# The taps of a short convolution, laid out once per partition by the host

## The chip, the cores and the metric

One core of one Trainium2 chip runs the program. The metric is device time in microseconds for one execution of the whole program, as the median of several runs. Preparing the input arrays on the host is not part of it.

## The reference

The sequence has 2048 positions of 576 channels. Two kinds of layers alternate, each of them twice, and each adds its result to its input. The first kind is a Fourier mixing over channels and positions; the second is a short causal convolution of four taps over the keys, a product with the values, a long causal convolution (2048 taps for each channel) and a gate. Everything is in 32-bit floats.

```python
def _A_ref(x, dft_seq_re, dft_seq_im, dft_hid_re, dft_hid_im):
    a = jnp.einsum("bsd,ed->bse", x, dft_hid_re)
    b = jnp.einsum("bsd,ed->bse", x, dft_hid_im)
    return jnp.einsum("ts,bse->bte", dft_seq_re, a) - jnp.einsum("ts,bse->bte", dft_seq_im, b)

def _B_ref(q, k, v, shift_k, ssm_k, ssm_D):
    k_pad = jnp.pad(k, ((0, 0), (ks - 1, 0), (0, 0)))
    k_shift = jnp.zeros_like(k)
    for t in range(ks):                       # ks = 4
        k_shift = k_shift + k_pad[:, t:t + S, :] * shift_k[:, ks - 1 - t][None, None, :]
    kv = k_shift * v
    ...                                       # y: long convolution of kv with ssm_k
    y = y + kv * ssm_D[None, None, :]
    return q * y

x = x + _A_ref(_layernorm(x), ...)
x = x + _B_ref(_layernorm(x), B_k, B_v, B_shift_k, B_ssm_k, B_ssm_D)
x = x + _A_ref(_layernorm(x), ...)
x = x + _B_ref(_layernorm(x), B_k, B_v, B_shift_k, B_ssm_k, B_ssm_D)
```

## The kernel before

The long convolution's result does not depend on the layers' input, only on the keys, the values and the filters. So the kernel computes it once, in pieces, beside the matrix products of the first Fourier layer.

**The Fourier layer.** `layer` walks over steps: for each of four blocks of 512 output positions, for the real and the imaginary matrix, and for each of 16 blocks of 128 input positions, one step. A step takes a 256 KB slice of the sequence matrix (`load_c`, issued through `load_after`, line 159, on SP's queue two steps ahead), splits it into a high and a low part (ScalarE on line 91, VectorE on line 92), and multiplies it with one block of normalized rows: twelve matmuls into four PSUM accumulators named `s` and two into one named `rm`, all on line 74. The rows come from `get_x0`: a load on SP (line 646), statistics on VectorE (line 172) or ScalarE (lines 612 and 614), the scaling on ScalarE (line 182, or 639 from the ninth block on), and the split by `to_x` (line 186 on ScalarE, 188 and 189 on VectorE).

**The branch.** `branch` is a generator for the long convolution; the main loop takes pieces from it between the steps. Its first stage goes over 16 blocks of keys times values and 16 blocks of the filter. `f1_loads` fetches the blocks, `f1_split` splits one (lines 91 and 92), and `f1_products` multiplies it with a constant matrix: four groups of three matmuls, each into a bank of a ring of three (`bk`), each evicted by ScalarE (line 432) and, two at a time, stored from ScalarE's queue (line 433).

**The short convolution.** `convolve`, a generator inside `branch`, runs on VectorE: for each pair of blocks and each of the four taps one product (line 382), and from the second tap on a sum (line 387). The padded keys are loaded by `load_k` (line 361, 4,608 bytes a partition, a partition's rows 36,864 bytes apart). The taps are loaded once, by `load_w4` (line 353) when `convolve` is first asked for work: two loads of two taps each, on SP's queue. Their destination is a tile of 1,152 words on each of the 128 partitions, the same 4,608 bytes on each, because every partition needs all channels of both taps. The tile lies in the region named `f1f` in the profile. The taps then stay there for the whole first stage.

**What sets the order.** Each engine executes its own instructions in order, and the order is fixed when the program is built; semaphores make an instruction wait for its inputs and for the space it writes to. SP issues most loads, ScalarE's queue the stores, GpSimd's queue a few loads that convert a type. Loads that one queue issues are served in the order of issue, so a load that is served slowly holds up those behind it.

Of the kernel before, what the change touches and what calls it, by code (L numbers as in the profile page):

```python
# [15 lines left out]
P = 128  # L16
S = 2048
D = 576
# [46 lines left out]
def fnet_h3_kernel(ctx: ExitStack, tc: tile.TileContext, x, c_mat, w_re, w_im, k_pad, v, shift_k,  # L65
                   ssm_k, ssm_d, f1c, i2c, midc, out):
    nc = tc.nc
# [68 lines left out]
    def two(v):  # L136
        return v.rearrange("p (a n) -> p a n", a=2)
# [200 lines left out]
    def branch():  # L338
# [11 lines left out]
        def load_w4():  # L350
            for i in range(2):
                t = two(ring["wt"]())
                nc.sync.dma_start(t, bass.AP(tensor=shift_k.tensor, offset=shift_k.offset + 2 * i * D,
                                             ap=[[0, P], [D, 2], [1, D]]))
                wt.extend(t[:, i, :].unsqueeze(1).broadcast_to([P, 2, D]) for i in range(2))

        def load_k(upto):
# [15 lines left out]
        def convolve():  # L373
            for i in range(J // 2):
                if not wt:
                    load_w4()
                load_k(i + KR - 1)
                rp = rows[i] = two(ring["rp"]())
                for t in range(4):
                    out_t = two(tmp) if t else rp  # L380
                    for n, k in k_rows(2 * i + t):
                        nc.vector.tensor_tensor(out_t[:, n], k, wt[3 - t][:, n], OP.mult)
                    yield
                    if t == 1:
                        load_k(i + KR)
                    if t:
                        nc.vector.tensor_tensor(rp, rp, out_t, OP.add)
                        yield
# [716 lines left out]
```

## Time and profile before

| | |
|---|---|
| median of three runs | 1205.37 us (1202.85, 1205.37, 1206.05) |
| span of the profiled execution | 1202.1 us |
| mean granted TensorE clock | 0.997 |
| DMA, mean over the span | 218 GB/s, 261.95 MB |
| SP's queue (q1), share of 16 engines | 53.2% |
| ScalarE's queue (q10), share of 16 engines | 10.2% |
| tap loads | 2 of 576.0 KB each, from SP |

The span runs from the first to the last instruction of one profiled execution; all times in the profile count from its start. The median stands 3.3 us above it. In the rows of the windows, columns name the busy time and number of instructions of each engine in a stretch, then the clock that TensorE was granted as a share of full speed, the mean busy share of the 16 DMA engines (above 1 where packets overlap) and the rate. In rows of the timeline, the brackets give the engine's idle time before the instruction and what ended it. `PEld` are TensorE's weight loads; `q` behind an engine's name is its sequencer, which issues DMAs. Durations of matmuls in the timeline are modelled and overlap; the chain of waits does not count an overlap twice.

### The profile page before, as it was taken

How to read it: one execution, taken by the hardware profiler on the slowest of the kernel's cores; microseconds unless marked ns; L12 is line 12 of the kernel's file. 1: busy time of each engine (PE TensorE's matmuls, PEld its weight loads, DVE VectorE, ACT ScalarE, POOL GpSimd, SP SyncE). 2: the span in 40 equal slices, each digit the busy share in tenths (PEclk: the TensorE clock that was granted, in tenths of full speed). 3: DMA queues.
4: the chain of work that ended last, by engine and by line, in shares of the span. 5: the costliest groups of instructions: out<-in, count | busy, mean ns of one | idle time of the engine just before them, and what ended most of it. 6: DMA issues, size and time to landing. Idle time of an engine off the chain costs nothing.

```text
span 1202.1 us, 18251 instructions
## 1 busy us (share of the span) xinstructions
PE 1181.4 (98%) x6320; PEld 1026.7 (85%) x6320; DVE 840.0 (70%) x1498; ACT 666.5 (55%) x1335; POOL 74.1 (6%) x116
## 2 busy tenths in 40 slices
PE   7999999999999999999999999999999999999997
PEld 5888888988888888888988898888888888789997
DVE  7899983678777677675347766775776777774764
ACT  6965665669877768675435666544444445450210
POOL 2200000000000000001101121000000000001111
PEclk9999999999999999999999999999999999999999
DMA  9879898546656666648967686872682686794621
GB/s 337 288 235 306 289 295 260 180 139 178 216 178 200 211 180 202 189 147 244 307 204 237 221 257 211 272 266 72 215 283 71 205 286 220 265 352 143 219 95 40
DMA packets 146110, 261.95 MB, mean 218 GB/s; under 512 B 15841, under 2 KB 44769, under 8 KB 146018
## 3 DMA queue, kind: packets, MB, share of 16 engines
q1 hardware_dynamic: 102674, 205.58, 53.2%
q10 hardware_dynamic: 36432, 42.63, 10.2%
q0 software_dynamic: 6912, 12.59, 3.9%
q8 instruction: 49, 0.80, 0.3%
q14 instruction: 43, 0.35, 0.1%
HBM read 194.09 MB, written 66.65 MB: 217 GB/s over the span
## 4 chain that ended last, share of the span: by engine, by line
PE 89%; DMA 3%; DVE 3%; ACT 3%; issue 1%; SPq 0%; POOLq 0%; ACTq 0%; POOL 0%; DVEq 0%
PE s L74 51%; PE bk L74 33%; PE rm L74 5%; DMA flts<-in_c_mat 1%; ACT flts L486 1%; DMA t<-ud 1%; ACT mid L486 0%; DMA t<-flts 0%; DVE mid L492 0%; DMA flts<-vd 0%; DMA flts<-in_ssm_k 0%; ACT u L91 0%; ACT mats L91 0%; DVE flts L172 0%; DVE mats L92 0%
## 5 line engine op out<-in xcount | busy, mean ns | idle before, releaser
L74 PE MATMUL s<-mats 128*128 128x512 f32 x2088 | 530.4, 392 | 0.4 <-DVE u L92 0.2
L74 PEld LDWEIGHTS s<-mats 128*128 128x128 f32 x2088 | 381.3, 188 | 70.6 <-DVE u L92 0.9
L92 DVE TENSOR_TENSOR mats<-flts,mats 128x512 fp32r<-128x512 f32 x206 | 141.1, 688 | 60.0 <-ACT mats L91 56.8
L91 ACT ACTIVATE mats<-flts 128x512 fp32r<-128x512 f32 x206 | 128.7, 627 | 86.4 <-PE bk L74 31.9
L74 PE MATMUL bk<-mid 128*128 128x288 f32 x768 | 131.2, 300 | 2.5 <-ACT flts L486 1.5
L74 PEld LDWEIGHTS bk<-mid 128*128 128x128 f32 x768 | 114.3, 188 | 22.1 <-ACT flts L486 9.0
L492 DVE TENSOR_TENSOR mid<-flts,mid 128x576 fp32r<-128x576 f32 (+1 forms) x160 | 101.9, 637 | 33.8 <-ACT mid L486 29.5
L74 PE MATMUL bk<-w,u 128*128 128x288 f32 x864 | 120.8, 295 | 0.1
L74 PEld LDWEIGHTS bk<-w,u 128*128 128x128 f32 x864 | 117.3, 188 | 3.6 <-ACT flts L486 1.2
L486 ACT ACTIVATE flts<-bk 128x288 f32<-128x288 f32 x160 | 61.9, 404 | 86.2 <-PE bk L74 69.8
L74 PE MATMUL rm<-mats 128*128 128x512 f32 x304 | 94.8, 390 | 0.0
L486 ACT ACTIVATE mid<-flts 128x576 fp32r<-128x576 f32 (+1 forms) x159 | 87.0, 582 | 7.5 <-DMA flts<-t 3.0
L486 ACT ACTIVATE flts<-flts 64x288 f32<-64x288 f32 x192 | 85.0, 443 | 5.9 <-ACT flts L486 0.4
L432 ACT ACTIVATE flts<-bk 128x288 f32<-128x288 f32 x128 | 49.4, 409 | 46.6 <-PE bk L74 40.1
L74 PE MATMUL bk<-f1r 128*128 128x288 f32 x384 | 66.0, 305 | 8.7 <-ACT f1r L91 6.8
L74 PEld LDWEIGHTS bk<-f1r 128*128 128x128 f32 x384 | 60.3, 194 | 16.0 <-ACT f1r L91 7.3
L74 PE MATMUL bk<-mats 128*128 128x288 f32 (+1 forms) x376 | 67.8, 317 | 0.0
L74 PEld LDWEIGHTS rm<-mats 128*128 128x128 f32 x304 | 56.9, 188 | 12.0 <-DVE flts L264 0.3
L278 DVE TENSOR_TENSOR flts<-flts,bk 128x288 f32<-128x288 f32 x48 | 21.7, 453 | 63.2 <-PE bk L74 63.2
L74 PE MATMUL s<-t,mats 128*128 128x512 f32 x264 | 65.5, 389 | 0.4 <-DVE t L92 0.4
L175 POOL TENSOR_TENSOR flts<-flts 128x1 f32<-128x1 f32 x35 | 28.5, 816 | 524.9 <-DVE flts L174 524.9
L74 PE MATMUL bk<-mats,t 128*128 128x288 f32 (+1 forms) x368 | 59.3, 303 | 0.0
(143 smaller groups left out, 1490.3 us busy)
## 6 DMA issues: line engine op xcount, KB each, us to landing
flts<-in_c_mat SPq DMA_DIRECT2D x148, 256.0 KB, 3.6
ph<-in_c_mat SPq DMA_DIRECT2D x54, 512.0 KB, 4.2
t<-flts ACTq DMA_DIRECT2D x64, 288.0 KB, 4.6
flts<-t SPq DMA_DIRECT2D x64, 288.0 KB, 2.9
flts<-in_c_mat SPq DMA_DIRECT2D x30, 512.0 KB, 4.9
vd<-flts ACTq DMA_DIRECT2D x64, 144.0 KB, 2.3
flts<-vd SPq DMA_DIRECT2D x32, 288.0 KB, 4.8
mid<-in_i2c POOLq DMA_DIRECT2D x32, 256.0 KB, 5.1
```

Source lines behind the costliest of these rows:

```text
L74: nc.tensor.matmul(ps, lhsT, rhs, start=first, stop=last, skip_group_check=more)
L91: a = nc.scalar.activation(h, src, AF.Copy).ins
L92: return a, nc.vector.tensor_tensor(l, src, h.bitcast(F32), OP.subtract).ins
L175: pows.append(nc.gpsimd.tensor_tensor(rs, ve, mhalf, OP.pow).ins)
L278: added[:] = [nc.vector.tensor_tensor(r[:, cs], r[:, cs], ps[:, :HD], OP.add).ins]
L432: stored[:] = [nc.scalar.activation(so[:, c, :], ps[:, :HD], AF.Copy).ins]
L486: last_act.append(nc.scalar.activation(*args, **kw).ins)
L492: nc.vector.tensor_tensor(l, src, h.bitcast(F32), OP.subtract)
```

## The change

The host passes the taps as an array of 128 x 4 x 576 words, in which the 4 x 576 taps stand once for each partition (1,179,648 bytes in place of 9,216). Each of the two loads then reads, for each partition, that partition's own 4,608 bytes, 9,216 bytes apart, where it read the same 4,608 bytes for all partitions. What lands in the tile is the same, and so are the number of loads, their queue, their place in it and the bytes that they move. On all five engines the instructions stand in the same order as before.

```diff
         def load_w4():
             for i in range(2):
                 t = two(ring["wt"]())
-                nc.sync.dma_start(t, bass.AP(tensor=shift_k.tensor, offset=shift_k.offset + 2 * i * D,
-                                             ap=[[0, P], [D, 2], [1, D]]))
+                nc.sync.dma_start(t, shift_k[:, 2 * i:2 * i + 2, :])
                 wt.extend(t[:, i, :].unsqueeze(1).broadcast_to([P, 2, D]) for i in range(2))
...
-        "shift_k": a["B_shift_k"].T,
+        "shift_k": np.broadcast_to(a["B_shift_k"].T, (P, 4, D)),
```

## The prediction

> **What bounds the kernel now.** I read the page first, then who TensorE waits for, then the chain of waits for the first 120 us, and last the DMA around the two changed loads. The page:
>
> ```profile
> span 1202.1 us, 18251 instructions
> ...
> PE 1181.4 (98%) x6320; PEld 1026.7 (85%) x6320; DVE 840.0 (70%) x1498; ACT 666.5 (55%) x1335; POOL 74.1 (6%) x116
> ...
> PE 89%; DMA 3%; DVE 3%; ACT 3%; issue 1%; SPq 0%; POOLq 0%; ACTq 0%; POOL 0%; DVEq 0%
> ```
>
> TensorE sets the end: 98% busy, 89% of the chain that ended last. A load can only buy time where TensorE stands still or runs slowly because of it. The list of what TensorE waited for (total us, times, longest) has one place of any size after the start:
>
> ```profile
> PE bk L74 <- ACT f1r L91: 6.8, 1, 6.8
> PE bk L74 <- ACT flts L432: 1.9, 1, 1.9
> ```
>
> The 6.8 us lie ahead of the first matmul, and the taps are asked for long after that. The 1.9 us are these two rows of TensorE's timeline (start, length, idle time before), and the windows show what else was lost there (columns: PE, PEld, DVE, ACT, POOL busy, granted clock, DMA share, GB/s):
>
> ```profile
> 27.66 0.61 PE L74 MATMUL rm<-mats 128*128 128x512 f32 x2
> 30.14 3.40 PE L74 MATMUL bk<-f1r 128*128 128x288 f32 x12 [1.86 <-ACT flts L432]
> ```
>
> ```profile
> 24.00:34.00 10.00, 8.10 (x35) 6.67 (x34) 8.46 (x16) 6.77 (x16) 0.55 (x1) 0.83 0.98 377
> 34.00:130.00 96.00, 96.00 (x484) 81.70 (x484) 88.08 (x132) 64.97 (x143) 13.30 (x17) 1.00 0.87 282
> 31.00:32.00 1.00, 0.99 (x4) 0.99 (x5) 1.00 (x4) 0.78 (x3) 0.00 (x0) 0.50 1.04 422
> ```
>
> TensorE idles 1.86 us (28.27 to 30.14) and right afterwards runs at clock 0.50; the mean of 0.83 over ten microseconds is 10 x 0.17 = 1.7 us of full-speed work lost. Together 3.56 us, all that this corner can give back. From 34 to 130 us it is busy without a gap, at clock 1.00. The chain of waits names the cause:
>
> ```profile
> 19.15 8.66 DMA flts<-in_c_mat
> ...
> 28.37 0.67 ACT mats L186
> 29.04 0.76 ACT early L182
> ...
> 31.01 2.53 PE bk L74 x9
> 33.54 1.15 PE s L74 x4
> ```
>
> A 256 KB slice of the sequence matrix, the sixth (step 5, counted from 0), is issued at 19.15 and lands at 27.81. ScalarE runs in order, so everything behind its rounding waits:
>
> ```profile
> 24.70 0.87 ACT L182 ACTIVATE early<-early,flts 128x576 f32<-128x576 f32 x1 [1.45 <-DVE flts L181]
> 27.84 0.63 ACT L91 ACTIVATE mats<-flts 128x512 fp32r<-128x512 f32 x1 [2.26 <-DMA flts<-in_c_mat]
> 28.95 0.85 ACT L182 ACTIVATE early<-early,flts 128x576 f32<-128x576 f32 x1
> 29.70 0.39 ACT L432 ACTIVATE flts<-bk 128x288 f32<-128x288 f32 x1
> 31.91 0.69 ACT L432 ACTIVATE flts<-bk 128x288 f32<-128x288 f32 x2
> 32.49 0.63 ACT L91 ACTIVATE mats<-flts 128x512 fp32r<-128x512 f32 x1
> ```
>
> ScalarE idles 2.26 us; the eviction at 29.70 (L432), queued behind the slice, is what frees the PSUM bank that TensorE wants at 28.27.
>
> **What the slice waits behind.** The tap loads:
>
> ```profile
> L353 SPq DMA_DIRECT2D f1f<-in_shift_k x2: 328/490/653, 17.8 to 20.2; - x2
> ...
> DMA to landing us min/median/max: 6.1/6.1/6.1
> ```
>
> The first, issued at 17.8, stands ahead of the slice in SP's queue. Its landing is 17.8 + 6.1 = 23.9. The DMA in half microseconds around it (the last two columns):
>
> ```profile
> 19.00:19.50 0.50, 0.50 (x3) 0.40 (x3) 0.50 (x2) 0.50 (x1) 0.00 (x0) 1.00 1.29 422
> 19.50:20.00 0.50, 0.50 (x4) 0.38 (x3) 0.50 (x3) 0.50 (x2) 0.00 (x0) 1.00 1.60 347
> 20.00:20.50 0.50, 0.50 (x4) 0.42 (x3) 0.50 (x3) 0.50 (x2) 0.00 (x0) 1.00 1.02 179
> 20.50:21.00 0.50, 0.50 (x5) 0.46 (x4) 0.40 (x2) 0.25 (x1) 0.32 (x1) 1.00 0.64 122
> 21.00:21.50 0.50, 0.50 (x4) 0.44 (x3) 0.23 (x2) 0.41 (x1) 0.23 (x1) 1.00 1.75 157
> 21.50:22.00 0.50, 0.50 (x4) 0.39 (x3) 0.50 (x4) 0.49 (x1) 0.00 (x0) 1.00 0.28 28
> 22.00:22.50 0.50, 0.50 (x4) 0.42 (x3) 0.50 (x2) 0.50 (x2) 0.00 (x0) 1.00 0.74 221
> 22.50:23.00 0.50, 0.50 (x4) 0.42 (x3) 0.50 (x3) 0.50 (x2) 0.15 (x1) 1.00 0.98 396
> ```
>
> The rate falls from 422 to between 28 and 221 GB/s and is back at 396 GB/s by 22.5. It is no lack of work: transfers issued before 20 us are still outstanding. SP's queue in 20 to 22 us and in 24 to 26 us (packets, MB, share of 16 engines' time):
>
> ```profile
> q1 hardware_dynamic: 48, 0.22, 89.1%
> ```
>
> ```profile
> q1 hardware_dynamic: 255, 0.81, 101.9%
> ```
>
> 0.891 x 16 x 2 us over 48 packets is 594 ns a packet; 1.019 x 32 over 255 is 128 ns. Packets differ in size, so take bytes: 130 against 40 us of engine time per MB. The first tap load is slow while it is served, and what sets it apart is that 128 partitions fetch one and the same 4,608 bytes.
>
> **The change part by part.** No instruction is added, dropped or moved; both loads carry 589,824 B before and after, by the same queue. Every step has the same issue cost, so the sum is made of waiting alone.
>
> Term 1, the DMA. Six half-microseconds at 347, 179, 122, 157, 28, 221 GB/s sum to 1,054; at 400 they would be 2,400. The deficit, 1,346 x 0.5 us = 673 KB, is 1.68 us at 400 GB/s (1.6 at 380, 1.75 at 420). If private rows stream like other loads, everything queued behind lands 1.68 us earlier: the slice at 26.13. The bounds are 0, should sharing not be the brake, and 1.75.
>
> Term 2, the gap. ScalarE takes the slice at 26.13 instead of 27.84, since it is idle then; the eviction moves from 29.70 to 28.0 and TensorE restarts at 28.46 instead of 30.14. The gap shrinks from 1.86 to about 0.2 us.
>
> Term 3, the clock. With a gap of 0.2 us I take the half-speed stretch as gone. Not all of its 1.7 us returns. The twelve matmuls at 30.14 are four groups of three on a ring of three banks, and the fourth needs the first of the two evictions at 31.91, which moves with ScalarE to 30.23 and ends at 30.6. Nine matmuls took 2.53 us at half clock, so three take 0.42 at full clock: step 5 starts at 31.0 instead of 33.54, 2.5 us earlier.
>
> The Trainium skill speaks against this term: TensorE: Matmul & The Clock Gate (Part 1) describes a clock that falls only after an idle window of about 3.4 us. Here it fell after 1.86 us of idling, so the trace does not agree; by that rule the gap would not be the cause of the half clock, and the saving would be term 2 alone.
>
> Term 4, what keeps it. ScalarE and VectorE are 1.68 us early, TensorE 2.5. Where their lead over TensorE is thin, TensorE waits for them. The thinnest row I found is step 13 (VectorE's second half of the slice, then the chain's first matmuls of that step):
>
> ```profile
> 60.17 0.68 DVE L92 TENSOR_TENSOR mats<-flts,mats 128x512 fp32r<-128x512 f32 x1
> ```
>
> ```profile
> 61.68 2.72 PE s L74 x12
> ```
>
> Ready at 60.85, used at 61.68: a lead of 0.83, so TensorE can be at most 1.68 + 0.83 = 2.5 us earlier. Behind 130 us I assume that a lead stays, since TensorE sets the end there. Sum: 2.5 us, bounds 0 and 3.56. The profiled span would become 1199.6. The timed runs (median 1205.37) lie 3.3 us above this span; I take the difference as it is, so 1202.9.
>
> The second tap load (20.2) I cost at nothing. It is served between the slice, landed at 27.81, and a row tile issued just behind it, at 20.93, that lands 10.3 us later, at 31.2:
>
> ```profile
> 20.93 0.71 SPq L646 DMA_DIRECT2D early<-in_x  x1
> 21.73 0.59 SPq L159 DMA_DIRECT2D flts<-in_c_mat  x1
> ```
>
> ```profile
> early<-in_x SPq DMA_DIRECT2D x1, 288.0 KB, 10.3
> ```
>
> ```profile
> 28.00:30.00 2.00, 0.28 (x2) 0.00 (x0) 1.07 (x4) 2.00 (x5) 0.00 (x0) 1.00 1.05 394
> ```
>
> The engines kept 394 GB/s in that stretch. So the second shared read shows no deficit, which is the strongest evidence against term 1: sharing cannot be enough by itself.
>
> [...]
>
> **Rivals.**
> - **The half clock stays** or comes back elsewhere. For: the gap was only 1.86 us, so idling in small pieces may be enough. Against: clock 1.00 from 34 to 130 us, with TensorE as loaded. Only term 2 is left: 1205.4 - 1.7 = 1203.7.
> - **All of the loss returns**, because later waits shrink too: 1205.4 - 3.56 = 1201.8. Against: the thin leads of term 4.
> - **The change does not do what it says**: the first load was slow for a reason other than sharing, as the second load's rate suggests. Then 1205.4.
> - **Private rows are slower**: 128 pieces spread over 1.18 MB instead of 4.6 KB. Suppose both loads run at the 121 GB/s that the four rows from 20 to 22 us average: 589,824 B take 4.9 us instead of 1.5, 3.4 too long each. The first already costs 1.68, so the slice comes 1.7 later; the next slice, issued at 21.73, lies behind both and comes 5.1 later. It landed 10.0 us after its issue,
>
> ```profile
> flts<-in_c_mat SPq DMA_DIRECT2D x1, 256.0 KB, 10.0
> ```
>
> at 31.7, and was wanted at 32.49, so 5.1 - 0.8 = 4.3 us reach TensorE: 1209.7. It decides as soon as the two loads together cost 0.8 us more than now. Against: the load of the padded key rows right behind the first tap load also fetches 4,608 B a partition from places of their own, and the rate is back at 396 GB/s with it.
>
> **How the numbers follow.** Forecast (2.5 us) 0.47, half clock stays 0.15, all returns 0.12, no effect 0.15, private rows slower 0.11. The likeliest gives 1202.9. About 0.3% (3.6 us) is what a measurement of this kernel can tell from no change; the three runs alone spread over 3.2 us. So the forecast itself reads as no change unless the medians fall apart by another 1.1 us: of its 0.47 I put 0.17 beyond the bound, with 0.10 from all returns and 0.03 from the rest: faster 0.30. Slower is the last rival and a little chance: 0.12. The same: 0.58. The range goes from 1199.5 (all returns and the run-to-run spread) to 1207.0 (no effect, and the spread upwards); it leaves out most of the last rival.
>
> **What would show it.** Term 1: no half microsecond under 300 GB/s between 19.5 and 22.5, and the slice landing by about 26.2. Term 2: the idle time ahead of the twelve matmuls under 0.5 us. Term 3: clock 1.00 in 30 to 34 us, step 5 starting at 31. Term 4: TensorE's later steps about 2.5 us earlier, still so at 130 us and at the end. A dip that stays, at the same place, would make the forecast wrong from its first term; a slice that lands early while the end does not move would fault term 4.

## The result and the profile after

| | before | with the change |
|---|---|---|
| median of 20 runs each | 1204.39 us (1202.85 to 1207.61) | 1203.05 us (1201.38 to 1206.01) |
| ratio of the two | | 0.9985, 95% interval 0.9978 to 0.9992 |
| span of the profiled execution | 1202.1 us | 1201.7 us |

The medians lie 1.3 us apart. The ratio, which is not the plain quotient of the two medians, stands for 1.8 us, with an interval of 1.0 to 2.6 us. That is the direction of the forecast and half to three quarters of its 2.5 us, and it lies inside the 0.3% that was called no change. The page of the changed kernel reads almost as before:

```profile
span 1201.7 us, 18251 instructions
...
PE 1181.4 (98%) x6320; PEld 1026.7 (85%) x6320; DVE 839.9 (70%) x1498; ACT 666.0 (55%) x1335; POOL 75.3 (6%) x116
...
PE 84%; DVE 5%; ACT 4%; DMA 4%; issue 2%; POOL 1%; SPq 0%; ACTq 0%; POOLq 0%; DVEq 0%
```

TensorE is busy for the same 1181.4 us, and its share of the chain that ended last is smaller (84% after 89%): some other engine holds it up more often. The page can't say where, so look at the corner that the prediction spoke of. The DMA in half microseconds (last column GB/s):

```profile
19.50:20.00 0.50, 0.50 (x4) 0.42 (x3) 0.50 (x2) 0.50 (x2) 0.00 (x0) 1.00 1.10 409
20.00:20.50 0.50, 0.50 (x4) 0.42 (x3) 0.50 (x3) 0.50 (x2) 0.00 (x0) 1.00 1.10 447
20.50:21.00 0.50, 0.50 (x4) 0.42 (x3) 0.50 (x3) 0.50 (x2) 0.00 (x0) 1.00 1.08 442
21.00:21.50 0.50, 0.50 (x4) 0.42 (x3) 0.41 (x2) 0.50 (x1) 0.32 (x1) 1.00 0.94 378
21.50:22.00 0.50, 0.50 (x4) 0.42 (x4) 0.23 (x2) 0.03 (x1) 0.23 (x1) 1.00 1.05 424
22.00:22.50 0.50, 0.50 (x5) 0.46 (x4) 0.50 (x4) 0.40 (x2) 0.00 (x0) 1.00 0.98 396
```

The dip to 28 GB/s is gone; no half microsecond is under 378. ScalarE's rounding of the slice of step 5, and the eviction behind it, in its timeline:

```profile
26.09 0.63 ACT L91 ACTIVATE mats<-flts 128x512 fp32r<-128x512 f32 x1
...
28.06 0.39 ACT L431 ACTIVATE flts<-bk 128x288 f32<-128x288 f32 x1
```

26.09 without a wait, where it was 27.84 after a wait of 2.26. (One line fewer in the program: L432 is now L431.) TensorE's timeline and the windows of the two stretches:

```profile
28.76 0.62 PE L74 MATMUL rm<-mats 128*128 128x512 f32 x2
29.22 1.80 PE L74 MATMUL bk<-f1r 128*128 128x288 f32 x12
30.85 1.10 PE L74 MATMUL s<-mats 128*128 128x512 f32 x4
```

```profile
24.00:34.00 10.00, 10.00 (x53) 8.65 (x52) 9.56 (x21) 8.58 (x20) 1.90 (x3) 1.00 0.94 345
34.00:130.00 96.00, 95.01 (x478) 80.11 (x477) 87.67 (x130) 63.37 (x138) 13.27 (x17) 1.00 0.86 281
```

The twelve matmuls follow without idle time, at clock 1.00 (0.15 us each, 0.28 before), and step 5 starts at 30.85 instead of 33.54. The second row is the new thing: from 34 to 130 us TensorE was busy for all of 96.00 us before, and now for 95.01. Three waits in its timeline make up this 1.00 us:

```profile
48.41 2.57 PE L74 MATMUL s<-mats 128*128 128x512 f32 x10 [0.18 <-DVE mats L92]
71.58 3.05 PE L74 MATMUL s<-mats 128*128 128x512 f32 x12 [0.59 <-DVE u L92]
86.20 0.53 PE L74 MATMUL bk<-f1r 128*128 128x288 f32 x2 [0.23 <-ACT f1r L91]
```

They lie in steps 10, 16 and 19: there TensorE now arrives before VectorE or ScalarE is done. The product that step 10 waits for is this row of VectorE, before and with the change:

```profile
48.83 0.68 DVE L92 TENSOR_TENSOR mats<-flts,mats 128x512 fp32r<-128x512 f32 x1
```

```profile
47.67 0.68 DVE L92 TENSOR_TENSOR mats<-flts,mats 128x512 fp32r<-128x512 f32 x1
```

VectorE is only 1.16 us early there, TensorE 2.74. The chain of waits, which before led through the slice's load at 19.15 us, now leads through VectorE, GpSimd and ScalarE up to 71.58 us (step 16) and again from 83.51 to 86.20 (step 19). TensorE's earlier start at step 5 is not on it.

How much of the lead survives is read from the last `rm` matmuls of a step, which end it. First the kernel before, steps 5, 25 and 43, then the changed kernel:

```profile
36.86 0.39 PE L74 MATMUL rm<-mats 128*128 128x512 f32 x1
...
117.71 0.62 PE L74 MATMUL rm<-mats 128*128 128x512 f32 x2
...
205.12 0.62 PE L74 MATMUL rm<-mats 128*128 128x512 f32 x2
```

```profile
34.12 0.39 PE L74 MATMUL rm<-mats 128*128 128x512 f32 x1
...
116.85 0.61 PE L74 MATMUL rm<-mats 128*128 128x512 f32 x2
...
204.26 0.62 PE L74 MATMUL rm<-mats 128*128 128x512 f32 x2
```

Step 5 ends 2.74 us earlier, step 25 0.86, step 43 still 0.86, and the span is 0.4 shorter. So 1.88 us of the gain are given back between steps 5 and 25, nearly all of it in the steps of the three waits: the lead is 2.74 us at the end of step 9 and 2.25 at the end of step 10, and 2.25, 1.47 and 1.02 at the ends of steps 15, 16 and 19. The profile names 1.00 of it as waits; the rest does not show as idle time (the ends of matmuls are modelled, so short waits can hide in them).

Late in the program the chain of waits shows where more is lost. Both kernels wait there for a load that brings back a stored block (`t` from `ud`), before and with the change:

```profile
1044.43 6.72 DMA t<-ud
```

```profile
1043.32 7.38 DMA t<-ud
```

It is issued 1.11 us earlier but takes 0.66 longer, so it lands 0.45 earlier. What TensorE has won until then counts only as far as this load lets it.

One more difference between the two executions has nothing to do with the taps: TensorE reaches the corner 1.1 us later in the second (step 4 ends at 28.76 + 0.62 = 29.38, before at 28.27). It starts slowly and turns to full speed at another time in each execution. The same eight matmuls of the first steps, in the kernel before, in the changed kernel, and in a second profile of the changed kernel (e10 below):

```profile
10.89 2.01 PE L74 MATMUL s<-mats 128*128 128x512 f32 x8
```

```profile
11.96 2.60 PE L74 MATMUL s<-mats 128*128 128x512 f32 x8
```

```profile
12.05 3.40 PE L74 MATMUL s<-mats 128*128 128x512 f32 x8
```

From the end of step 4 to the end of step 5 the kernel before takes 8.98 us (28.27 to 37.25) and the changed one 5.13 (29.38 to 34.51): the corner itself gives 3.85 us, of which the later arrival hides 1.1.

### The profile page after: what moved, and what is told of

Its sections match the earlier page's. It is cut to its first block, busy times and chain, and to the rows that moved or that the text cites. A ratio compares the mean times of both kernels' runs of the same rounds, so it can differ in the third digit from the quotient of the medians.

```text
span 1201.7 us, 18251 instructions
## 1 busy us (share of the span) xinstructions
PE 1181.4 (98%) x6320; PEld 1026.7 (85%) x6320; DVE 839.9 (70%) x1498; ACT 666.0 (55%) x1335; POOL 75.3 (6%) x116
## 4 chain that ended last, share of the span: by engine, by line
PE 84%; DVE 5%; ACT 4%; DMA 4%; issue 2%; POOL 1%; SPq 0%; ACTq 0%; POOLq 0%; DVEq 0%
PE s L74 46%; PE bk L74 33%; PE rm L74 5%; ACT flts L485 1%; DMA flts<-in_c_mat 1%; DVE mats L189 1%; DMA t<-ud 1%; DVE mats L92 1%; DVE f1f L386 1%; DMA t<-flts 1%; ACT mid L485 1%; ACT mats L91 1%; POOL flts L615 0%; DVE f1f L381 0%; DMA flts<-in_ssm_k 0%
## 5 line engine op out<-in xcount | busy, mean ns | idle before, releaser
L74 PE MATMUL s<-mats 128*128 128x512 f32 x2088 | 531.4, 392 | 1.3 <-DVE u L92 0.8
L74 PEld LDWEIGHTS s<-mats 128*128 128x128 f32 x2088 | 381.7, 188 | 71.9 <-DVE u L92 1.7
L74 PE MATMUL bk<-mid 128*128 128x288 f32 x768 | 131.2, 300 | 1.7 <-ACT flts L485 0.9
L74 PEld LDWEIGHTS bk<-mid 128*128 128x128 f32 x768 | 114.3, 188 | 21.3 <-ACT flts L485 8.4
L74 PE MATMUL bk<-w,u 128*128 128x288 f32 x864 | 120.8, 296 | 0.4 <-DVE w L232 0.4
L74 PEld LDWEIGHTS bk<-w,u 128*128 128x128 f32 x864 | 117.3, 188 | 4.1 <-ACT flts L485 1.3
L74 PE MATMUL rm<-mats 128*128 128x512 f32 x304 | 94.9, 391 | 0.0
L431 ACT ACTIVATE flts<-bk 128x288 f32<-128x288 f32 x128 | 49.2, 409 | 47.1 <-PE bk L74 40.0
L74 PE MATMUL bk<-f1r 128*128 128x288 f32 x384 | 64.9, 301 | 7.2 <-ACT f1r L91 7.2
L74 PEld LDWEIGHTS bk<-f1r 128*128 128x128 f32 x384 | 59.8, 192 | 14.2 <-ACT f1r L91 7.6
L74 PE MATMUL bk<-mats 128*128 128x288 f32 (+1 forms) x376 | 67.8, 317 | 0.0
L74 PEld LDWEIGHTS rm<-mats 128*128 128x128 f32 x304 | 56.9, 188 | 12.1 <-DVE flts L264 0.3
L74 PE MATMUL s<-t,mats 128*128 128x512 f32 x264 | 65.5, 390 | 1.6 <-DVE t L92 1.6
L74 PEld LDWEIGHTS s<-t,mats 128*128 128x128 f32 x264 | 49.5, 188 | 12.2 <-DVE t L92 2.0
```

The source lines that it names most:

```text
L74: nc.tensor.matmul(ps, lhsT, rhs, start=first, stop=last, skip_group_check=more)
L431: stored[:] = [nc.scalar.activation(so[:, c, :], ps[:, :HD], AF.Copy).ins]
```

## The experiments

e4, which holds loads alone, is not in the table. The column "at or under 0.997" counts runs whose mean granted clock was no higher than that; one stretch of 3.4 us at half clock costs 1.7 us, 0.0014 of the span.

| kernel | runs | median us | ratio to before | at or under 0.997 |
|---|---|---|---|---|
| the change | 20 | 1203.05 | 0.9985 (0.9978 to 0.9992) | 1 |
| e1, both loads shared, large array | 12 | 1204.27 | 1.0005 (0.9993 to 1.0018) | 4 |
| e2, load issued first shared | 12 | 1203.21 | 0.9988 (0.9977 to 1.0) | 2 |
| e3, load issued second shared | 11 | 1202.60 | 0.9988 (0.9977 to 0.9998) | 0 |
| e5, change + one copy ahead of the slice | 11 | 1202.14 | 0.9980 (0.9970 to 0.9991) | 2 |
| e6, change + two copies | 11 | 1205.88 | 1.0008 (0.9996 to 1.0020) | 3 |
| e7, two taps left out | 12 | 1202.87 | 0.9983 (0.9972 to 0.9994) | 2 |
| e8, e7 + two copies | 11 | 1204.03 | 0.9989 (0.9980 to 0.9999) | 4 |
| e9, before again | 12 | 1204.13 | 1.0002 (0.9990 to 1.0014) | 6 |
| e10, the change again | 12 | 1202.29 | 0.9993 (0.9982 to 1.0003) | 1 |
| e11, change, taps asked for later | 12 | 1203.44 | 0.9997 (0.9982 to 1.0011) | 0 |
| e12, before's loads, taps asked for later | 12 | 1203.55 | 1.0003 (0.9993 to 1.0012) | 0 |

Each ratio is to runs of the kernel before on the same chip: e1 to e3 share 29 of them (median 1203.94), e5 to e8 35 (1205.37), e9 to e12 35 (1203.49). Ratios of different groups are compared, not times.

### e1: the large array, read as before

```diff
-                nc.sync.dma_start(t, shift_k[:, 2 * i:2 * i + 2, :])
+                nc.sync.dma_start(t, bass.AP(tensor=shift_k.tensor, offset=shift_k.offset + 2 * i * D,
+                                             ap=[[0, P], [D, 2], [1, D]]))
```

> The host's larger array is there, but both loads read its first copy for all partitions, as before the change. Theory (sharing is the brake): as before the change: half microseconds under 250 GB/s between 19.5 and 22.5 us, the sixth slice landing at about 27.8, an idle gap of TensorE of 1.5 to 2 us and time within 0.1% of before. Rival (the array's size or place in memory, not the sharing): no dip, slice at about 26, time 0.1 to 0.2% under before.

Measured: no faster than before (1.0005). The dip is there, in windows of its profile, though smaller:

```profile
20.00:20.50 0.50, 0.50 (x4) 0.41 (x3) 0.50 (x3) 0.50 (x2) 0.00 (x0) 1.00 0.75 243
20.50:21.00 0.50, 0.50 (x4) 0.41 (x3) 0.50 (x3) 0.50 (x2) 0.00 (x0) 1.00 0.60 237
21.00:21.50 0.50, 0.50 (x5) 0.46 (x5) 0.28 (x1) 0.23 (x2) 0.44 (x1) 1.00 1.02 313
```

With the next two half microseconds (332 and 359) it lacks 258 KB against 400 GB/s, 0.65 us, where the kernel before lacked 673 KB. The slice is rounded at 26.25, TensorE hardly waits, and the clock stays at 1.00 in this profile. So the size and place of the array are not the cause of the gain. What is new is that the same shared loads cost 1.68 us in one execution and 0.65 in another, by the rate.

### e2 and e3: one load private, the other shared

A point about order first: the load of taps 2 and 3 (`i = 1`) is issued ahead of that of taps 0 and 1. So in e2, where `i = 0` is private, the load issued first is the shared one, and in e3 the load issued first is private. "First" and "second" in the expectations follow the code, so they are the wrong way round as to time.

```diff
-                nc.sync.dma_start(t, shift_k[:, 2 * i:2 * i + 2, :])
+                nc.sync.dma_start(t, <shared> if i else shift_k[:, 2 * i:2 * i + 2, :])    # e2
+                nc.sync.dma_start(t, shift_k[:, 2 * i:2 * i + 2, :] if i else <shared>)    # e3
```

> Only the first tap load reads private rows; the second reads shared rows of the same array. Theory (only the first shared load costs anything): no dip, the sixth slice lands by 26.2, time as with the change (0.1 to 0.2% under before). Rival (both shared loads cost): a dip moves to the second load, about 673 KB of missing transfer at 23 to 28 us, and the time is that of before.

> Only the second tap load reads private rows; the first reads shared rows. Theory: the dip of 600 to 750 KB at 19.5 to 22.5 us stays, the half clock too, and the time is that of before within 0.1%. Rival (the second load matters): at least half of the gain of the change.

Measured: 0.9988 for both, which neither tells them apart nor from the change. By the prediction's account e2, with the shared load ahead of the slice, should have been as slow as before; its interval goes up to 1.0000, so it only leans against that. In e2 the deficit is 148 KB (332, 230 and 341 GB/s from 20.5 to 22.0), in e3 134 KB (342, 290, 359 and 341 from 19.0 to 21.0). So a dip of this size comes with a private load ahead of the slice too; e7 below, also private, lacks 173 KB (335, 226 and 293 from 19.0 to 20.5). In e3 another 260 KB are missing from 25.0 to 27.5, where e2 lacks nothing; that this is its second, shared load was not followed. e3's TensorE timeline has a wait all the same:

```profile
27.62 0.61 PE L74 MATMUL rm<-mats 128*128 128x512 f32 x2
29.02 0.66 PE L74 MATMUL bk<-f1r 128*128 128x288 f32 x3 [0.79 <-ACT flts L432]
29.89 1.63 PE L74 MATMUL bk<-f1r 128*128 128x288 f32 x9 [0.21 <-ACT flts L432]
```

It idles for 0.79 us and goes on at full clock (0.18 us a matmul). The times don't say which of the two loads matters.

### e4: shared reads by themselves

Groups of eight loads of 589,824 B, each partition 4,608 B, closed by one small VectorE instruction that waits for all eight and holds back the next group. Groups differ in the distance between the rows of neighbouring partitions.

```python
for words in (9216, 0, 64, 256, 576, 1152, 2304, 0):
    for i in range(8):
        nc.sync.dma_start(at(i), bass.AP(tensor=k_pad.tensor, offset=k_pad.offset, ap=[[words, P], [1, W]]))
    close()
...   # then the taps' private rows, then private and shared loads in turn
```

> The layers are left out: ten groups of eight loads of 4,608 bytes a partition from the padded keys or the taps, each group closed by one small instruction, with distances between partitions of 9216, 0, 64, 256, 576, 1152, 2304 and 0 words, then the taps' private rows, then shared and private loads in turn. Theory (rows shared by all partitions are slow when all engines are on them): the groups at 0 words run at 150 to 250 GB/s, the others from 576 words on at 380 or more, those at 64 and 256 words between; the alternating group near 300. Rival (sharing as such is not slow; the first load was slow for what surrounded it): all groups within 5% of each other at 380 to 420 GB/s.

VectorE's timeline; the idle time in brackets is the length of a group:

```profile
32.08 0.18 DVE L27 TENSOR_TENSOR buf<-buf 128x8 f32<-128x8 f32 x1 [16.80 <-DMA buf<-in_k_pad]
46.01 0.18 DVE L27 TENSOR_TENSOR buf<-buf 128x8 f32<-128x8 f32 x1 [13.75 <-DMA buf<-in_k_pad]
...
120.57 0.18 DVE L27 TENSOR_TENSOR buf<-buf 128x8 f32<-128x8 f32 x1 [16.81 <-DMA buf<-in_k_pad]
134.79 0.18 DVE L27 TENSOR_TENSOR buf<-buf 128x8 f32<-128x8 f32 x1 [14.05 <-DMA buf<-in_shift_k]
150.10 0.18 DVE L27 TENSOR_TENSOR buf<-buf 128x8 f32<-128x8 f32 x1 [15.13 <-DMA buf<-in_k_pad]
```

The two shared groups take 16.80 and 16.81 us. Neighbours 64 words apart take 13.75 (the second row), larger distances 13.87 to 14.72, the taps' private rows 14.05, and the mixed group 15.13. So sharing is a brake by itself, twice to a hundredth of a microsecond: (16.8 - 14.05) / 8 = 0.34 us a load. The start of the first such group, in its windows (the last column is GB/s):

```profile
17.00:18.00 1.00, 0.00 (x0) 0.00 (x0) 1.00 1.00 415
18.00:19.00 1.00, 0.00 (x0) 0.00 (x0) 1.00 1.00 406
19.00:20.00 1.00, 0.00 (x0) 0.00 (x0) 1.00 1.31 180
20.00:21.00 1.00, 0.00 (x0) 0.00 (x0) 1.00 0.73 226
21.00:22.00 1.00, 0.00 (x0) 0.00 (x0) 1.00 0.99 323
```

It starts at full rate, slumps to 180 GB/s, and goes on at some 330 up to 31 us. That is less harm than expected, and much less than 1.68 us for one load. Overlapping rows (64 words) are as good as separate ones, so the copy for each partition is more than the cure needs.

### e5 and e6: the slice made late on purpose

One or two memory-to-memory copies of 589,824 B go into SP's queue between the first tap load and the slice, in the changed kernel.

```diff
+    pad_d = [dr.tile([P, 2 * D], F32, name=f"pad{m}") for m in range(1)]    # e6: range(2)
...
                 nc.sync.dma_start(t, shift_k[:, 2 * i:2 * i + 2, :])
+                if i == 1:
+                    for m in range(1):    # e6: range(2)
+                        anchor.append(load_after(pad_d[m], k_pad[m * J:m * J + 2 * P, :].rearrange("(p a) d -> p (a d)", a=2)))
```

> The change, with a copy of 589,824 B from one place in memory to another put into SP's queue ahead of the sixth slice: a stall made on purpose. Theory (a late slice stalls TensorE and drops its clock): the slice lands 1.5 to 2 us later than with the change (at about 28), TensorE idles 1 to 2 us, most runs show a clock of 0.997 or less, and the median is 1.5 to 3 us over the change's 1203.05. Rival (what a late slice costs is given back, since the other engines' leads set the pace up to 110 us): within 0.7 us of the change.

> As the stall before, with two such copies; the scheduler also puts the second tap load ahead of the slice. Theory: the slice lands 4 to 5 us later than with the change, TensorE idles 3 to 5 us, the clock is at 0.997 or less in all runs, the median is 3.5 to 6 us over 1203.05. Rival: less than 2 us over it.

e5 is no slower than the change (0.9980). Its ScalarE and TensorE rows:

```profile
28.92 0.39 ACT L435 ACTIVATE flts<-bk 128x288 f32<-128x288 f32 x1
29.21 0.62 ACT L91 ACTIVATE mats<-flts 128x512 fp32r<-128x512 f32 x1
```

```profile
32.47 0.50 PE L74 MATMUL s<-mats 128*128 128x512 f32 x1 [0.44 <-DVE mats L92]
```

The slice is rounded at 29.21, 1.4 us later than in the kernel before, and TensorE waits for only 0.44 us. The reason is in the first row: with the copy added, the order that is fixed when the program is built has two evictions (L435 here; 28.06 and 28.92) ahead of the rounding on ScalarE. So e5 is not the old stall again at another size. It suggests, unasked, that a late slice alone hardly stops TensorE (0.44 us here), and that an eviction queued behind it does. This profile has a half clock too, but at 220 us, after waits of 1.67 and 0.47 us long behind the tap loads.

In e6, where the order is changed in the same way, the idle pieces are larger, the clock stays at 1.00 there, and it costs 0.0023 over the change, 2.8 us, between the theory and the rival:

```profile
30.59 0.66 PE L74 MATMUL bk<-f1r 128*128 128x288 f32 x3 [1.17 <-ACT flts L435]
31.46 3.52 PE L74 MATMUL bk<-f1r 128*128 128x288 f32 x21 [0.22 <-ACT flts L435]
...
37.78 2.11 PE L74 MATMUL s<-mats 128*128 128x512 f32 x8 [1.58 <-DVE mats L92]
```

Step 5 ends at 40.11, 5.6 us later than with the change. But by then TensorE has done 48 matmuls of the branch and with the change 38, and ten of them take 1.5 us (0.15 each), so the delay is some 4.1 us. Step 25, with 164 such matmuls done in both, ends at 120.44, 3.0 later. So about a quarter of a delay at this corner is caught up, and the rest reaches the end.

### e7 and e8: a lighter VectorE

If VectorE's thin leads are what takes the gain back, the lead should stay when VectorE has less to do. Two of four taps lose their product and sum; e8 has e6's two copies as well.

```diff
                 for t in range(4):
+                    if t > 1:
+                        yield
+                        yield
+                        continue
```

> The change, with the products and sums of the third and fourth tap left out, so that VectorE has 32 instructions of 1.35 us less up to 110 us. Theory (VectorE's thin lead is what takes back the time won at step 5): TensorE reaches step 25 earlier than with the change (117.5 us) by 0.8 us or more, and the median is 0.8 to 2.5 us under 1203.05. Rival (the lead is lost to something else): within 0.5 us of the change in both.

> The lighter VectorE of the run before with the two copies of the larger stall. Theory: nothing absorbs the stall now, so the difference to the light kernel without it, at step 25 and in the medians, is as large as the delay at step 5 (3 us or more), and larger than the same difference with the full VectorE work. Rival: the difference is the same with and without the work.

Up to step 25 e7 goes as expected: it ends it at 115.96, 1.5 us before the change does. Then its TensorE timeline has

```profile
124.94 1.06 PE L74 MATMUL bk<-f1r 128*128 128x288 f32 x6 [1.43 <-ACT flts L435]
```

and step 30 ends at 143.10, 0.7 us behind the change's 142.36. e8 ends step 5 at 38.83, 3.6 us after e7, of which ten more matmuls of the branch are 1.5; so the delay is some 2.1 us, and at step 25 (118.25) it is 2.3: nothing is caught up up to there. Step 30 ends at 143.16, level with e7. In the medians the theory failed: e7 is level with the change (0.9983 and 0.9985), and e8 lies 0.0006 above e7, less than the 0.0023 between e6 and the change. So VectorE alone is not what takes the lead back: where it has less to do, ScalarE's evictions hold TensorE a little later. That part of the theory fell.

### e9 and e10: both kernels again

No edit; both profiled again on one chip, to see how much of the picture belongs to one execution.

> The kernel before, unchanged, profiled a second time. Theory (the shared load costs every time, but its cost differs from run to run, and only the long ones stall TensorE into the half clock): the dip is there again with a deficit between 100 and 673 KB; a third or more of the runs have a mean clock of 0.997 or less. Rival (the first profile shows what every run does): a deficit of 600 KB or more, an idle gap of 1.5 us or more, a stretch at clock 0.50 near 30 us.

> The kernel with the change, unchanged, profiled a second time, on the same chip as the run of before. Theory: no dip, no half clock near 30 us, at most 15% of the runs at a mean clock of 0.997 or less, median 0.5 to 2.5 us under before. Rival: the difference of the first comparison was chance, and the interval holds 1.000 with its middle above 0.9995.

e9 shows the stall again, from a dip of 462 KB (194 to 369 GB/s from 19.0 to 23.0):

```profile
31.07 0.67 PE L74 MATMUL bk<-f1r 128*128 128x288 f32 x3 [2.09 <-ACT flts L432]
...
24.00:34.00 10.00, 7.71 (x36) 6.36 (x36) 8.23 (x17) 6.10 (x14) 0.94 (x2) 0.91 0.97 365
```

e10 shows neither dip nor wait (`30.11 1.79 PE L74` for the twelve matmuls). Step 5 ends at 35.37 against 38.46, 3.1 us earlier, and step 25 at 118.33 against 120.48, 2.15 earlier. e10 has the same three waits at steps 10, 16 and 19, 1.15 us together. The medians differ by 1.8 us, the intervals overlap, and that of e10 (0.9982 to 1.0003) holds 1.000: the repetition alone would not show the gain.

### e11 and e12: the slices ahead of the taps

The convolution begins one block later, so that the slices of steps 5 and 6 stand ahead of the tap loads in SP's queue. e11 has the private rows, e12 the shared ones.

```diff
-                if later and n > 1:
+                if later and n > 2:
```

> The change, and the short convolution is begun one block later, which puts the sixth and the next slice ahead of the tap loads in SP's queue. Theory: the sixth slice lands before 24 us, TensorE has no gap there, and the median is at or up to 1.5 us under the change's. Rival: the convolution's later start uses up VectorE's thin lead, and the median is more than 1 us over the change's.

> The same later start with the shared tap loads of before. Theory (the shared reads matter only through the slice behind them): within 0.05% of the run with private rows and the same start. Rival (shared reads cost by themselves wherever they stand): 1 us or more slower than that run.

The two differ by 0.1 us in the medians and by 0.0006 in the ratios, each known to 0.0010 or 0.0015. That agrees with shared reads that cost nothing where no urgent load is queued behind them, but does not show it: a cost of 1 us could hide, and in e12's profile the shared loads were not slow at all (no half microsecond from 17 to 33 us is under 302 GB/s). Neither is faster than before. In e11 the slice is rounded at 23.47 and step 5 ends at 31.77, 2.7 us before the change does, but some 2 us of that are 14 matmuls of the branch that come later there (24 up to that point, with the change 38). Step 25, with the same work done, ends at 118.07, 0.6 after the change. Its timeline says why:

```profile
86.33 0.53 PE L74 MATMUL bk<-f1r 128*128 128x288 f32 x2 [1.56 <-ACT f1r L91]
```

TensorE runs into step 19 again, and there the delayed convolution is now late.

No version beats the change by more than its interval.

## Why the prediction was right in kind and too large

**The mechanism held.** Shared rows slow the load (e4); in both profiles of the changed kernel the dip from 19.5 to 22.5 us is gone, the slice comes at 26.09 in the first (forecast 26.13), the wait and the half clock go, and step 5 starts at 30.85 (forecast 31.0). That these times come so near is in part luck: the slice was also issued 0.22 us earlier in this execution, and TensorE came 1.1 later. e1 rules out the array itself. That the path to the time leads through the loads queued behind agrees with e12 and is otherwise argued from the traces. The rivals of a half clock that stays and of slower private rows are out: the clock is 1.00 there in both profiles of the changed kernel, and private rows take 14.05 us for eight loads against 16.8. The rival of no effect is out by the 20 runs of each kernel and by e1.

**Term 1 was mis-sized: one execution's dip was taken for every execution's.** With a shared load ahead of the slice, four profiles lack 673, 462, 258 and 148 KB, which is 1.68, 1.15, 0.65 and 0.37 us at 400 GB/s. e4's mean, 0.34 us, is at the low end. And e3 and e7, with a private load there, lack 134 and 173 KB. The time from the slice's issue to its landing separates the two kinds better. Before and with the change:

```profile
flts<-in_c_mat SPq DMA_DIRECT2D x1, 256.0 KB, 8.7
```

```profile
flts<-in_c_mat SPq DMA_DIRECT2D x1, 256.0 KB, 7.1
```

With a shared load ahead it is 8.7 us (before and e9), 8.0 (e2) and 7.2 (e1), with a private one 7.0 to 7.2 (the change, e10, e3 and e7). So sharing held the slice up by 1.7 us at most and in one execution not at all. I had a sign of it, the second shared load without a deficit, and priced it as a chance that sharing is not the cause. It meant that the cost varies.

**Terms 2 and 3 were right for a run in which the stall occurs, and it does not always occur.** In the seven profiles with the same order of instructions, TensorE can restart 2.3 us after the rounding of the slice begins (before: 27.84 and 30.14). Whether it waits depends on when it gets there, and that moves with its slow start:

| profile | slice rounded | +2.3 us | step 4 done | wait | half clock after |
|---|---|---|---|---|---|
| before | 27.84 | 30.14 | 28.27 | 1.86 | yes |
| e9, before again | 28.77 | 31.07 | 28.98 | 2.09 | yes |
| e1 | 26.25 | 28.55 | 28.67 | none | no |
| e2 | 26.79 | 29.09 | 29.07 | none | no |
| e3 | 26.71 | 29.01 | 28.23 | 0.79 | no |
| change | 26.09 | 28.39 | 29.38 | none | no |
| e10, change again | 26.91 | 29.21 | 30.28 | none | no |

It is a race between two times that both vary from run to run: the issue of the slice (18.81 to 20.03 us) and its way through the queue set one, the slow start the other. In e3 TensorE has to wait with a private load ahead. The timed runs fit the race. Of the runs with both loads shared in their old place (the three groups of before, e9 and e1), 49 of 123 have a mean clock of 0.997 or less; of e2's, with only the load ahead of the slice shared, 2 of 12, which fits less well; of e3's none of 11; of those of the changed kernel 2 of 32; of e12's, where the slice is ahead of the shared loads, none of 12. In the three groups the runs of before at 0.997 have medians of 1205.5, 1205.5 and 1205.5, those at 0.998 of 1203.0, 1204.4 and 1203.2, so some 2 us lie between. A share smaller by 34 points (40% against 6%) times 2 us is 0.7 us, about half of the 1.3 measured. On the chip of e5 to e8 such runs are more frequent altogether, with the same contrast: 20 of 35 for before, 4 of 23 for e5 and e7. Without that chip before (with e9) and e1 have 29 of 88, and the estimate becomes 0.5 us. This last step is worked out, not shown, for the clock of a timed run does not say where it fell. Of the five stretches of 3.4 us at half clock that the profiles show between the slow start and the last matmul, two lie at step 5 (before, e9), two behind the late load of `t` (e9 at 1056 us, e8 at 1053) and one at 220 us (e5), so two of them in kernels with private rows.

**Term 4 failed.** It put the cap at step 13, from a lead of 0.83, took VectorE as 1.68 us early, and assumed that the lead then stays. Step 13 was the thinnest row I had looked at, not the thinnest there is, and VectorE was 1.16 us early at step 10. The changed kernel waits in steps 10, 16 and 19, for VectorE twice and ScalarE once, and 2.74 us at step 5 become 0.86 at step 25; in the second pair 3.1 become 2.15. From there on the lead does stay, up to step 43 at least. That TensorE sets the end behind 130 us was wrong at the load of `t` near 1044 us: a lead of 1.11 there becomes 0.45. The list of waits before already had TensorE waiting 0.4 and 1.0 us there. The span came out at 1201.7, not at 1199.6. That makes "all of the loss returns" wrong too, although the corner itself gave 3.85 us, a little more than its 3.56.

**The base.** The three runs shown had a median of 1205.37, the 20 of the comparison 1204.39. That the forecast of 1202.9 lies so near the measured 1203.05 is luck: a gain 1.2 too large was taken from a base 1.0 too high.

The half clock after 1.86 us had spoken against the Trainium skill's TensorE: Matmul & The Clock Gate (Part 1), which has the clock fall after an idle window of about 3.4 us. e9 repeats it after 2.09 us, so the measurements decide against that threshold here. The length of the stretch, 3.4 us in both profiles, does agree with the window which that page gives for getting back to full speed.

**What stays open.** Why the dip of the same shared load differs by a factor of more than 4 between executions, and why it exceeds e4's 0.34 us by so much in some. What share of the measured gain comes from step 5. Where in steps 10, 16 and 19 the part of the given-back lead hides that no wait shows. How long an idle time drops the clock: it fell after 1.86 and 2.09 us at step 5, after 2.20 and 0.59 close together (e9) and 2.84 (e8) behind the late load, and after 1.67 and 0.47 close together (e5); it did not fall after 0.79, nor after 1.17, 0.22 and 1.58 in e6, nor after 1.59 and 0.42 at the late load with the change. A smaller offset between partitions instead of full copies was tried in e4 only, not in the kernel.

## What to carry to other kernels

When all partitions read the same rows, look at what the queue holds behind that load: here the cost came through the slice behind it and the eviction behind the slice. Before a stall in a profile is priced as a gain, ask whether it depends on a race, and compare the clock and span of several runs, since one profile shows one outcome. And a lead won on the busiest engine is kept only as far as the thinnest lead of the engines that feed it: go through all steps behind the corner, not to the first thin one.

## What the runs showed of the hardware beside that

- TensorE ran at half clock for 3.4 us after an idle time of only 1.86 and 2.09 us. The clock fell 0.3 us after the matmuls had begun again in the first case (30.5 after 30.14), and 1.2 us after it in the second (32.3 after 31.07).
- Its slow start ends at different times: the same eight matmuls took 2.01, 2.60 and 3.40 us in three executions, and step 4 ended between 28.2 and 30.3 us in kernels with the same order of instructions.
- Shared rows start at full rate (415 GB/s), slump (180) and then go on at about 330 in the first group of e4; a distance of 64 words between partitions, so that rows still overlap almost wholly, restores the rate (13.75 us against 16.80 for eight loads).
